# Weight sums in two steps, their loads reordered, and a remainder copy on one engine: a change at the start of a dilated-convolution kernel

## The chip, the cores and the metric

The kernel runs on one core of a Trainium2 chip. The metric is the device time in microseconds (us) of one execution. The engines that compute are TensorE (PE in the profile; PEld is its weight load), VectorE (DVE), ScalarE (ACT) and GpSimd (POOL). SP is the queue from which most DMAs are issued; ACT and POOL issue some as well.

## The reference

A causal convolution with 15 taps at distance 2, from 144 to 288 channels, over two sequences of 16000 steps, then a gate and a projection:

```
xp = pad(x, 28 steps in front)
h  = sum over i of  xp[:, 28 - 2i : 28 - 2i + T, :] @ w[i]      # w: 15 x 144 x 288
z  = tanh(h[..., :144]) * sigmoid(h[..., 144:])
out = z @ w_o                                                   # w_o: 144 x 144
```

All arrays are bf16.

## The kernel before, in words

The channels are split into 128, which fill TensorE's rows, and a remainder of 16. For the 128, the kernel uses a fast-convolution scheme: sums and differences of shifted inputs (tiles S, D, E and their further sums S2, S4, S42, E2, E4 and so on, made by VectorE, L316) are multiplied with sums and differences of weights (tiles G1, Gm, H, HH, GD), so that fewer products are needed. The stationary operand of a matmul is an input tile, the moving operand a weight tile of 288 columns; every product of this kind is recorded at L491. The remainder channels are gathered into a tile R (for taps 0 to 7 and 8 to 14 at once) and multiplied with Wr.

Positions are cut into 11 blocks and 21 units. A unit does four products called S, D, F and G; each has steps VV (with HH), V2 (with H), AV (with GD, for S and D) and A (with the taps themselves and the remainder). ScalarE moves sums between PSUM banks (L677, L683, L695, L761), VectorE combines them into y (L316), ScalarE gates (tanh and sigmoid, L744 and L746), VectorE multiplies (z), a DMA transposes z, and TensorE projects (OP0, OP1; evicted at L882). PSUM is used as four pairs of banks. The first unit's A products of the remainder are separate steps with an r at the end (A11Fr).

The order of every queue is written out by hand in the string ORDER: for PE, ACT, DVE, DMA (which is SP) and POOL, the steps in their order, as unit/name#number, with unit -1 for what is prepared before the first unit. A planner walks these lists and emits the instructions; the costs and due times (want) given to it only settle in which order the queues' instructions are interleaved in the program and which pair of banks each step gets. Instructions that stand in the code outside the planner, such as the clearing of the first xt, xn and Wr tiles on GpSimd (L336, L354, L376, L536), come ahead of all planned steps of their engine.

What matters for the change:

- **Warming.** L525 to L527: NWARM matmuls of 512 columns on zeros (wz), before any data is there.
- **Weight loads.** load_w (L529) loads the 128-channel part of w in four chunks q of four taps (three in the last), on SP, into w_all. Step w is chunk 0, w#1 chunk 1, w#2 chunk 2, w#3 chunk 3; ORDER has them as w, w#2, w#1, w#3, first on SP. After them come the first block's input in two halves (xn, xn#1, L343, transposing DMAs) and its remainder channels in three loads (xt, xt#1, xt#2, L384; the first one is 24 runs of 32 bytes into one partition), with the first xt between the two halves.
- **Weight sums.** For S, psum_sum (L560) adds weights on TensorE: matmuls of the weights with the identity or its negative into PSUM, and a ScalarE copy out (L572). G = w[j] + w[j+8]; H = G[j] - G[j+4]; HH and GD are further differences. Each sum is built directly from w, so HH takes up to eight matmuls for a column block; 59 matmuls in nine groups. For D, F and G the sums are made by VectorE (wsum, L550; instructions at L554).
- **Remainder of the first block.** sums_front (L403): VectorE's st sums (tile T), 16 transposes on TensorE per half block (trR, L420) into a pair of banks, then two copies into R, ScalarE's for one bank and VectorE's for the other (cpR, L427), then two matmuls that zero the banks (zR, L432). This is done twice, for the two units of the block.
- **Wr loads.** 15 loads of 9 KB on POOL (L540), mixed with the loads of w_o (L542, L547, L548) and the clearing of its tile (L544).
- **The end.** The last unit's gates (gate, L730) take smaller pieces: F's four columns at once (th8), then G's first two (th0), then columns 2 and 3 alone (th2, th3), with y made in two instructions for the latter (L788). All pieces under four columns use the start of the same th and sg tile. project_end (L816) transposes z on TensorE (L844), copies it (L855), projects it and evicts it (ose, L852; L830 for columns 4 to 7). store_last (L908) then stores twelve columns, each with a DMA of its own: columns 6 to 11 from POOL, 1 and 3 from ACT, 0, 2, 4 and 5 from SP.

Of the kernel before, what the change touches and what calls it, by code (L numbers as in the profile page):

```python
# [8 lines left out]
BF16 = mybir.dt.bfloat16  # L9
# [17 lines left out]
def t_dve(n, psum=False):  # L27
# [19 lines left out]
   V2bD A00S A01S VVF A00D A01D A10D A11D V2bF V2aF 8/OP0 9/VVG A01F A11F A00F A10F 10/AVS 9/V2bG V2aG 8/OP1 10/VVS 9/A01G A00G 10/AVD V2aS V2bS 9/A10G
   10/VVD 9/A11G 10/A01S V2aD V2bD A00S A10S A11S A11D VVF A10D A01D A00D V2aF V2bF 11/AVD 10/VVG A10F A00F V2aG A11F 9/OP1 10/A01F V2bG 9/OP0 11/VVS
   10/A10G A11G A01G A00G 11/V2aS V2bS AVS VVD A11S A10S V2bD V2aD A00S A01S VVF A10D A11D V2bF V2aF A01D A00D 10/OP0 11/A10F VVG A01F 12/AVS 11/A11F
   A00F V2aG V2bG 10/OP1 12/VVS 11/A00G A01G 12/AVD V2bS V2aS 11/A11G 12/VVD 11/A10G 12/A01S V2bD V2aD A00S A10S A11S A00D VVF A01D A11D A10D V2aF V2bF  # L50
   13/AVD 12/VVG A10F A01F A11F A00F V2bG V2aG 11/OP1 OP0 12/A11G 13/VVS 12/A10G 13/AVS V2bS V2aS 12/A00G 13/VVD 12/A01G 13/A11S V2aD V2bD A10S A00S
   A01S A00D A01D VVF A11D A10D 12/OP0 13/V2bF V2aF VVG 14/AVS 13/A01F V2aG A00F V2bG A10F A11F 12/OP1 13/A00G 14/VVS 13/A01G 14/AVD V2bS V2aS 13/A11G
   14/VVD 13/A10G 14/A01S A00S V2bD V2aD A10S A11S VVF A10D A11D A01D A00D V2bF V2aF 15/AVD 14/VVG A01F V2bG A10F V2aG A11F A00F A10G 13/OP1 OP0
   14/A11G 15/VVS 14/A00G A01G 15/V2bS V2aS AVS VVD A00S A01S V2bD V2aD A11S A10S VVF A10D A11D A00D A01D V2bF V2aF 14/OP0 15/VVG A01F A00F 16/AVS
   15/V2aG A10F V2bG 14/OP1 15/A11F A10G 16/VVS 15/A11G 16/AVD V2bS V2aS 15/A01G A00G 16/VVD A11S A10S V2bD V2aD A01S A00S VVF A10D A11D A01D A00D V2aF
   V2bF 17/AVD 16/VVG A00F V2aG V2bG A01F A11F A10F A00G A01G 15/OP1 OP0 17/VVS 16/A10G A11G 17/V2aS V2bS AVS VVD A11S A10S V2aD V2bD A01S A00S VVF
   A01D A00D A11D A10D V2aF V2bF 16/OP0 17/VVG A00F A01F A10F 18/AVS 17/V2aG V2bG A11F 16/OP1 17/A00G 18/VVS 17/A01G 18/AVD V2bS V2aS 17/A11G A10G
   18/VVD A10S A11S V2aD V2bD A01S VVF A00S A01D A00D A11D A10D V2aF V2bF 19/AVD 18/VVG A01F A00F A11F A10F V2aG V2bG 17/OP1 OP0 18/A00G 19/VVS 18/A01G
   19/AVS V2bS V2aS 18/A11G A10G 19/VVD A10S A11S V2bD V2aD A01S A00S VVF A11D A10D A00D A01D V2aF V2bF 18/OP0 19/VVG A10F A00F A01F 20/AVS 19/V2aG
   V2bG A11F 18/OP1 19/A00G 20/VVS 19/A01G A11G 20/AVD V2aS V2bS 19/A10G 20/VVD A00S V2bD V2aD A01S A11S A10S A01D A00D VVF A11D A10D V2bF V2aF VVG  # L60
   19/OP1 20/A01F A11F A10F V2bG V2aG A00F 19/OP0 20/A00G A01G OP0 OP1 tr#1 A10G A11G OPe#2 tr OPe#1 tr#2 OPe tr#3 tr#4 OPe#4 OPe#3 OPe#5
ACT:
   -1/wsum#7 wsum#13 wsum#5 wsum#11 wsum#17 wsum#9 wsum#3 hc wsum#1 0/cVVF -1/wsum#15 0/cVF cVVG -1/cpR 0/cVG y1F y0F y0G cVVS y1G eAVS cVS -1/cpR#2
   0/ev0S cVVD ev1S eAVD cVD 1/cVVS 0/ev0D 1/cVS 0/ev1D 1/ev0S cVVD eAVD ev1S cVD eAVS cVVF 0/th4 1/ev1D ev0D cVF 0/th0 1/cVVG 0/sg4 sg0 1/cVG 2/eAVS
   cVVS 1/th4 2/cVS 1/sg4 2/eAVD cVVD ev0S ev1S cVD 1/os0 2/cVVF ev1D ev0D cVF cVVG 3/eAVD 1/sg0 2/cVG 1/th0 os1 3/cVVS 2/th4 sg4 3/cVS cVVD eAVS ev1S
   cVD cVVF ev0S ev0D ev1D cVF 2/os0 3/cVVG 2/th0 4/eAVS 3/cVG 2/sg0 3/sg4 4/cVVS 3/th4 2/os1 4/cVS cVVD eAVD ev1S cVD cVVF ev0S ev0D ev1D cVF cVVG
   3/th0 sg0 5/eAVD 4/cVG 3/os1 os0 5/cVVS eAVS cVS 4/sg4 5/cVVD ev1S cVD ev0S cVVF ev0D ev1D cVF 4/os0 th4 th0 5/cVVG 6/eAVS 5/cVG 4/os1 6/cVVS 4/sg0
   5/sg4 6/cVS cVVD eAVD ev1S cVD cVVF ev0S ev1D ev0D cVF 5/th0 6/cVVG 7/eAVD 5/th4 sg0 6/cVG 5/os1 os0 7/cVVS eAVS cVS cVVD 6/sg4 7/cVD ev0S ev1S cVVF
   ev1D ev0D cVF 6/os0 7/cVVG 6/th0 8/eAVS 6/sg0 7/cVG 6/os1 8/cVVS 6/th4 8/eAVD cVS cVVD 7/sg4 8/ev0S cVD cVVF ev1S ev0D ev1D cVF 7/th4 th0 8/cVVG
   7/sg0 9/eAVD 8/cVG 7/os1 os0 8/th4 9/cVVS 8/sg4 9/cVS cVVD eAVS ev1S cVD ev0S cVVF ev0D ev1D cVF 8/sg0 os0 9/cVVG 8/th0 10/eAVS 9/cVG 8/os1 10/cVVS  # L70
# [174 lines left out]
def kernel(  # L245
# [8 lines left out]
    P = 128  # L254
# [148 lines left out]
    def sums_front(want):  # L403
# [7 lines left out]
        for r in range(2):  # L411
# [11 lines left out]
            for h, (eng, c) in enumerate((("ACT", t_act(8 * P)), ("DVE", t_dve(8 * P)))):  # L423
                def cp(h=h, pr=pr, R=R):
                    src = banks[pr.slot][:, h, 0:512].bitcast(BF16)
                    dst = R.tile[:, 2 * h:2 * h + 2].rearrange("p s k n -> p (s k n)")
                    K_(nc.vector.tensor_copy(out=dst, in_=src) if h else nc.scalar.copy(out=dst, in_=src))  # L427
# [569 lines left out]
```

## Time and profile before

| | us |
|---|---|
| Median of 3 runs | 313.51 (313.39 to 313.54) |
| The profiled execution | 313.12 |
| Its span, first to last instruction | 311.3 |
| TensorE busy | 297.5 (96%), 2604 matmuls |
| VectorE busy | 276.5 (89%) |
| ScalarE busy | 269.0 (86%) |
| GpSimd busy | 27.0 (9%) |

Busy time overlaps between engines, and a matmul's end is modelled, so a busy TensorE isn't TensorE at its peak. A timeline row gives the start, the length, the engine, the line, the operation with output and inputs, and in brackets how long the engine was idle before it and who ended that. SPq, ACTq and POOLq rows are issues of DMAs: their length is the time in which the queue was occupied by the issue, not that of the transfer. The stage table gives for each stretch of time the busy time of each engine, the granted clock of TensorE as a share of full speed, and the DMA engines' share.

### The profile page before, as it was taken

Reading aid. Unit: us, or ns where it says so; the run is one execution under the profiler, and the core shown is the slowest. Engines: PE = TensorE matmul, PEld = TensorE weight load, DVE = VectorE, ACT = ScalarE, POOL = GpSimd, SP = SyncE. Lnnn points to the kernel's source line nnn. Section 1 sums busy time; section 2 is a strip of 40 time slices with the busy share of each in tenths; the row PEclk is TensorE's granted clock in tenths of the full one; section 3 lists DMA queues with packets and bytes.
Section 4 is the critical chain, followed back from the end, with each engine's and each line's share of the span. In section 5 each row is a group of like instructions: output and inputs, shape, how many; then the busy total and the mean of one; then the engine's idle time right before and its main releaser. Section 6 shows DMA issues by size and latency. Waiting matters only on the chain.

```text
span 311.3 us, 6703 instructions
## 1 busy us (share of the span) xinstructions
PE 297.5 (96%) x2604; PEld 276.5 (89%) x2604; DVE 276.5 (89%) x393; ACT 269.0 (86%) x449; POOL 27.0 (9%) x63
## 2 busy tenths in 40 slices
PE   8998899999999999999999999999999999999981
PEld 3797789999999999999999999999999999999881
DVE  4878999999999999899999999989996998899861
ACT  1658789998989989999998999989888999989982
POOL 9830500000000000000000000000000000000013
PEclk9999999999999999999999999999999999999997
DMA  7995569597799866986796698455886647254344
GB/s 199 107 127 118 150 67 174 140 115 153 126 162 282 215 159 104 142 199 155 189 210 98 118 181 182 138 127 162 146 187 80 123 141 231 73 128 114 59 170 131
DMA packets 153110, 45.78 MB, mean 147 GB/s; under 512 B 137061, under 2 KB 151701, under 8 KB 153078
## 3 DMA queue, kind: packets, MB, share of 16 engines
q1 hardware_dynamic: 151610, 44.59, 69.6%
q0 software_dynamic: 1216, 0.70, 1.1%
q8 instruction: 20, 0.33, 0.5%
q14 instruction: 12, 0.10, 0.1%
q10 hardware_dynamic: 252, 0.06, 0.1%
HBM read 13.31 MB, written 11.84 MB: 81 GB/s over the span
## 4 chain that ended last, share of the span: by engine, by line
PE 80%; ACT 13%; DVE 3%; issue 3%; DVEq 0%; ACTq 0%
PE acc L491 77%; ACT m L761 4%; ACT acc L683 3%; PE acc L527 2%; ACT acc L677 1%; ACT sg L746 1%; ACT th L744 1%; ACT R L427 1%; DVE D L316 1%; DVE S L316 1%; PE acc L420 1%; DVE y L316 1%; ACT os L882 0%; ACT av L695 0%; ACT osl L852 0%
## 5 line engine op out<-in xcount | busy, mean ns | idle before, releaser
L491 PEld LDWEIGHTS <-E 128*128 128x128 bf16 x882 | 112.2, 145 | 7.9 <-issue 4.0
L491 PE MATMUL acc<-w_all,E 128*128 128x288 bf16 x630 | 101.2, 286 | 1.0 <-ACT acc L683 0.3
L491 PE MATMUL acc<-Wr,R 128*128 128x288 bf16 x336 | 94.9, 286 | 0.0
L316 DVE TENSOR_TENSOR y<-U,acc 128x576 bf16<-128x576 bf16 (+1 forms) x81 | 59.4, 744 | 9.9 <-PE acc L491 6.5
L683 ACT ACTIVATE acc<-acc 128x576 f32<-128x576 f32 x84 | 54.1, 645 | 7.2 <-PE acc L491 4.9
L761 ACT ACTIVATE m<-acc 128x576 bf16<-128x576 f32 x84 | 52.8, 651 | 4.3 <-PE acc L491 2.9
L491 PEld LDWEIGHTS <-S 128*128 128x128 bf16 x378 | 48.2, 137 | 5.2 <-issue 2.4
L491 PEld LDWEIGHTS <-D 128*128 128x128 bf16 x378 | 48.8, 137 | 4.0 <-issue 1.1
L677 ACT ACTIVATE acc<-acc 128x288 f32<-128x288 f32 x84 | 33.7, 401 | 8.0 <-PE acc L491 6.4
L746 ACT ACTIVATE sg<-y 128x576 bf16<-128x576 bf16 (+3 forms) x45 | 38.9, 872 | 0.5 <-DVE y L316 0.4
L744 ACT ACTIVATE th<-y 128x576 bf16<-128x576 bf16 (+3 forms) x45 | 38.9, 871 | 0.2
L882 ACT CAST os<-acc 128x864 bf16<-128x864 f32 x40 | 34.6, 880 | 2.0 <-DVE y L316 0.9
L316 DVE TENSOR_TENSOR m<-m,av 128x1152 bf16<-128x1152 bf16 x42 | 30.5, 753 | 6.5 <-ACT m L761 6.3
L491 PE MATMUL acc<-wo_ab,zT 128*128 128x144 bf16 x480 | 35.2, 226 | 0.1
L491 PEld LDWEIGHTS <-zT 128*128 128x128 bf16 x480 | 32.2, 98 | 1.5 <-issue 0.3
L491 PEld LDWEIGHTS <-R 128*128 128x128 bf16 x336 | 32.8, 98 | 0.2
L491 PE MATMUL acc<-G,S 128*128 128x288 bf16 x147 | 30.3, 286 | 0.4 <-ACT acc L683 0.2
L491 PE MATMUL acc<-Gm,D 128*128 128x288 bf16 x147 | 29.7, 285 | 0.3
L695 ACT ACTIVATE av<-acc 128x576 bf16<-128x576 f32 x42 | 27.2, 648 | 3.0 <-PE acc L491 2.4
L491 PE MATMUL acc<-H,E 128*128 128x288 bf16 x168 | 28.1, 286 | 1.1 <-ACT acc L677 1.1
L316 DVE TENSOR_TENSOR E<-E 128x1792 bf16<-128x1792 bf16 (+1 forms) x22 | 28.1, 1286 | 0.0
L316 DVE TENSOR_TENSOR z<-th,sg 128x576 bf16<-128x576 bf16 (+3 forms) x45 | 25.5, 573 | 2.1 <-ACT sg L746 1.4
(75 smaller groups left out, 330.0 us busy)
## 6 DMA issues: line engine op xcount, KB each, us to landing
R<-q SPq DMA_DIRECT2D x19, 512.0 KB
out_dram<-os SPq DMA_DIRECT2D x8, 864.0 KB
q<-T SPq DMA_DIRECT2D x10, 256.0 KB
out_dram<-os SPq DMA_DIRECT2D x2, 519.8 KB
xt<-in_x_dram SPq DMA_DIRECT2D x6, 156.0 KB
w_all<-in_w_dram SPq DMA_DIRECT2D x3, 288.0 KB
out_dram<-os SPq DMA_DIRECT2D x2, 337.5 KB
zT<-z SPq DMA_TRANSPOSE x20
```

What stands on the lines that cost most here:

```text
L316: return K_(nc.vector.tensor_tensor(out=out_, in0=a, in1=b, op=op))
L420: K_(nc.tensor.transpose(to, ap(st.tile, c, [1, P]), ident[:, 0, :]))
L427: K_(nc.vector.tensor_copy(out=dst, in_=src) if h else nc.scalar.copy(out=dst, in_=src))
L491: K_(nc.tensor.matmul(bank, lhsT=l(), rhs=r, start=start and q == 0, stop=end and q == len(jobs) - 1, skip_group_check=True))
L527: K_(nc.tensor.matmul(banks[i % 4][:, (i // 4) % 2, :], lhsT=wz[:, 0:P], rhs=wz[:], start=True, stop=True))
L677: add("ACT", t_act(D2), lambda: K_(nc.scalar.activation(out=banks[X.slot][:, 1, 0:D2], in_=banks[X.slot][:, 0, 0:D2], func=ACT.Copy, scale ...
L683: s = add("ACT", t_act(2 * D2), lambda: K_(nc.scalar.activation(out=banks[Y.slot][:, :, 0:D2], in_=banks[X.slot][:, :, 0:D2], func=ACT.Cop ...
L695: add("ACT", t_act(2 * D2), lambda: K_(nc.scalar.activation(out=av.tile[:, SPLIT.index(k)], in_=banks[W.slot][:, :, 0:D2], func=ACT.Copy, ...
L744: add("ACT", t_act(n * D, False), lambda: K_(nc.scalar.activation(out=a_, in_=y_[0], func=ACT.Tanh)), r=[*need, y], w=[th], want=t0, name= ...
L746: add("ACT", t_act(n * D, False), lambda: K_(nc.scalar.activation(out=b_, in_=y_[1], func=ACT.Sigmoid)), r=[*need, y], w=[sg], want=t0 + . ...
L761: add("ACT", t_act(2 * D2), lambda pair=pair, i=i, b2=b2: K_(nc.scalar.activation(out=m.tile[:, i, 2 * b2:2 * b2 + 2, :], in_=banks[pair.s ...
L882: K_(nc.scalar.copy(out=dst, in_=banks[pr.slot][:, :, 0:3 * D].rearrange("p h (q d) -> p h q d", d=D)))
```

## The change

- NWARM goes from 15 to 13.
- SP's order starts with the first xt of block 0, then weight chunks 1, 2, 0 and 3; then both halves of xn, one behind the other, then the other xt loads.
- The S sums are built in two steps. G comes first, from w (four groups, 14 matmuls); HH, H and GD are then built from G (five groups, 24 matmuls). Each group of the second step reads what ScalarE copied out in the first.
- VectorE's order at the start: the sums of Gm and H come in another order; ws#6, ws#2, ws#9, ws#7 and ws#10 stand between the first and the second half of E.
- The remainder's copy out of PSUM (cpR) is one VectorE instruction of 2048 elements instead of one of 1024 on each of ScalarE and VectorE.
- On POOL all 15 Wr loads come first, then the clearing and the loads of w_o.
- At the end: columns 2 and 3 of the last G come from one y instruction; gates of under four columns have parts of the th and sg tiles to themselves; column 7 is stored from SP instead of POOL.
- Costs for the planner change, and with them ORDER in all its lists: the middle has the same steps, in places in another order.

```diff
 PE:
-   -1/wsum#10 wsum#6 wsum#12 wsum#4 wsum#16 wsum#8 wsum#2 wsum wsum#14 0/VVF V2bF V2aF VVG -1/trR 0/V2aG V2bG A01F A11F -1/zR 0/A10F A00F A00G A11Fr
+   -1/wsum wsum#4 wsum#2 wsum#6 wsum#8 wsum#10 wsum#12 wsum#14 wsum#16 0/VVF V2bF V2aF VVG -1/trR 0/V2aG V2bG A11F A01F A00F -1/zR 0/A10F A00Fr A11Fr
+   A10Fr A01Fr A10G A01G A11G 1/AVS 0/A11Gr A10Gr A00G VVS A01Gr A00Gr AVS V2aS V2bS -1/trR#1 0/A10S A11S A00S A11Sr A10Sr A01S A00Sr A01Sr -1/zR#1
...
 ACT:
+   -1/wsum#1 wsum#5 wsum#7 wsum#3 hc wsum#11 wsum#9 wsum#13 wsum#15 0/cVVF -1/wsum#17 0/cVF cVVG cVG y0F y1F y1G cVVS y0G eAVS cVS ev1S ev0S cVVD eAVD
...
 DVE:
+   -1/ws ws#5 ws#1 ws#8 E ws#6 ws#2 ws#9 ws#7 ws#10 E#1 E2 ws#3 ws#11 stE stD stS E4 cpR S 1/stE -1/S4 1/stD -1/wr D S2 wr#1 ws#4 1/stS -1/S42 D2 cpR#1
...
 DMA:
-   -1/w w#2 w#1 w#3 xn xt xn#1 xt#1 xt#2 xt#3 xt#4 xt#5 0/xt -1/xn#2 1/T 0/xn 1/q R 2/xt 0/zT 4/xt#4 2/xn 3/T 1/R#1 3/q 1/zT 4/xn 5/T 6/xt#5 xt#2 3/R
+   -1/xt w#2 w#1 w w#3 xn xn#1 xt#1 xt#2 xt#3 xt#5 xt#4 0/xt -1/xn#2 1/T 0/xn 1/q 2/xt 1/R R#1 4/xt#4 0/zT 3/T q 2/xn 4/xt#5 1/zT 3/R#1 4/xt 5/T 6/xt#3
...
-            for h, (eng, c) in enumerate((("ACT", t_act(8 * P)), ("DVE", t_dve(8 * P)))):
...
+            def cp(pr=pr, R=R):
+                src = banks[pr.slot][:, :, 0:512].bitcast(BF16)
+                dst = R.tile[:].rearrange("p (h s) k n -> p h (s k n)", h=2)
+                K_(nc.vector.tensor_copy(out=dst, in_=src))
+
+            add("DVE", 0.07 + 16 * P / 1700, cp, r=[*pr.part], w=[R], pairs=[pr], want=want + 2 + 8 * r, name="cpR")
...
-    NWARM = 15
+    NWARM = 13
...
-    for q in range(4):
+    for q in (0, 2, 1, 3):
         load_w(q)
...
-        psum_sum(HH[:, i], [plus(i, j) + minus(i, j + 4) + minus(i, j + 2) + plus(i, j + 6) for j in range(2)], wall, [gHH[k]], wt)
-        psum_sum(H[:, i, 0:2], [plus(i, j) + minus(i, j + 4) for j in (0, 1)], wall, [gH[k]], wt + .2)
...
+        psum_sum(g[:, 0:2], [plus(i, j) for j in (0, 1)], wa, [gG[k, 0]], wt)
+        psum_sum(g[:, 4:6], [plus(i, j) for j in (4, 5)], wb, [gG[k, 1]], wt + .1)
+        psum_sum(g[:, 2:4], [plus(i, j) for j in (2, 3)], wa, [gG[k, 0]], wt + .2)
+        psum_sum(g[:, 6:7], [plus(i, 6)], wb, [gG[k, 1]], wt + .3)
+        of = lambda j: g[:, j, :] if j < 7 else w_all[:, 7, :]
+        both = [gG[k, 0], gG[k, 1], gw[1]]
+        psum_sum(HH[:, i], [[(0, of(j)), (1, of(j + 4)), (1, of(j + 2)), (0, of(j + 6))] for j in (0, 1)], both, [gHH[k]], wt + .4)
+        psum_sum(H[:, i, 0:2], [[(0, of(j)), (1, of(j + 4))] for j in (0, 1)], both, [gH[k]], wt + .5)
+        psum_sum(H[:, i, 2:4], [[(0, of(j)), (1, of(j + 4))] for j in (2, 3)], both, [gH[k]], wt + .6)
...
+            own = last and n < 4
+            th, sg = (Gen(v[8].gens[0]) if own else v[4 if n == 4 else 8].new(0) for v in (th_b, sg_b))
+            if own:
+                th.tile, sg.tile = (v[8].tiles[0][:, c0:c0 + n, :] for v in (th_b, sg_b))
...
-        store_last(c, os[c // 6], done_[c], len(units) * TU + 4 + q / 4, "POOL" if c > 5 else "ACT" if c in (1, 3) else "DMA")
+        store_last(c, os[c // 6], done_[c], len(units) * TU + 4 + q / 4, "POOL" if c in (6, 8, 9, 10, 11) else "ACT" if c in (1, 3) else "DMA")
```

204 lines of the change are left out of this document (97 added, 107 removed).

## The prediction

> **What bounds the kernel now.** I read the table by stage first, then the timelines of the first 30 us and the last 10, where the diff works.
>
> ```profile
> 26.50:39.75 13.25, 11.04 (x81) 9.40 (x80) 11.89 (x17) 10.59 (x21) 4.73 (x9) 1.00 0.75 151
> ...
> 66.25:278.25 212.00, 211.05 (x1887) 201.77 (x1886) 197.71 (x271) 195.43 (x321) 0.96 (x5) 1.00 0.74 156
> ...
> 303.80:307.20 3.40, 1.17 (x13) 0.62 (x10) 1.05 (x4) 1.60 (x6) 2.43 (x4) 1.00 0.71 224
> 307.20:311.30 4.10, 0.00 (x0) 0.00 (x0) 0.00 (x0) 0.00 (x0) 0.00 (x0) 0.51 0.16 36
> ```
>
> In this table (columns: stretch, length, busy PE, PEld, DVE, ACT, POOL, clock, DMA) TensorE is busy for 211.05 of 212.00 us from 66 to 278 us. There it is full: an edit that gives VectorE or ScalarE time back is worth nothing in that stretch, and a delay at the start is carried to the end unless the loose stages, 13 to 53 us, swallow it (2.2 us idle in 26.5 to 39.75 alone). So the question is when the start hands over to the full stretch. Four timelines of the start, by engine, tell what it waits for (columns: start, length, engine, line, operation, tiles, count, idle before it and who ended it):
>
> ```profile
> 1.19 6.20 PE L527 MATMUL acc<-wz 128*128 128x512 bf16 x15 [1.19 <-DVE wz L521]
> 7.23 7.39 PE L491 MATMUL acc<-w_all,ident 128*128 128x288 bf16 x59
> 14.46 0.41 PE L491 MATMUL acc<-HH,E 128*128 128x288 bf16 x2
> ...
> 17.64 1.14 PE L491 MATMUL acc<-w_all,E 128*128 128x288 bf16 x8
> 19.03 0.41 PE L432 MATMUL acc<-wz 128*128 128x288 bf16 x2 [0.25 <-DVE R L427]
> ```
>
> ```profile
> 0.74 2.11 SPq L531 DMA_DIRECT2D w_all<-in_w_dram  x4
> ...
> 5.65 0.94 SPq L384 DMA_DIRECT2D xt<-in_x_dram  x1
> ```
>
> ```profile
> 1.94 0.61 POOL L376 MEMSET xt<- 128x624 bf16 x1
> ```
>
> ```profile
> 5.87 0.76 DVE L554 TENSOR_TENSOR H<-w_all 128x1152 bf16<-128x1152 bf16 x1 [0.47 <-DMA w_all<-in_w_dram]
> 6.56 0.61 DVE L554 TENSOR_TENSOR Gm<-w_all 128x864 bf16<-128x864 bf16 x1
> 7.20 0.31 DVE L554 TENSOR_TENSOR GD<-Gm 128x288 bf16<-128x288 bf16 x1
> 7.43 0.60 DVE L554 TENSOR_TENSOR H<-w_all 128x864 bf16<-128x864 bf16 x1
> 7.95 0.45 DVE L554 TENSOR_TENSOR HH<-H 128x576 bf16<-128x576 bf16 x1
> 9.33 0.96 DVE L316 TENSOR_TENSOR E<-xn 128x1536 bf16<-128x1536 bf16 x1 [0.93 <-DMA xn<-in_x_dram]
> ...
> 12.29 1.09 DVE L316 TENSOR_TENSOR E<-E 128x1792 bf16<-128x1792 bf16 x1
> ...
> 14.49 0.76 DVE L316 TENSOR_TENSOR T<-xt 128x256 bf16<-128x256 bf16 x3 [0.37 <-issue]
> 15.18 1.48 DVE L316 TENSOR_TENSOR E<-E 128x2560 bf16<-128x2560 bf16 x1
> ```
>
> Now TensorE warms up, sums weights without a gap until 14.46, and the first unit's taps (w_all,E) follow at 17.64, behind the E sums of VectorE, which end at 16.66.
>
> **The loads: a moved step that stalls its queue.** The new order puts the first xt load of block 0 ahead of the weights on SP. It is small (24 runs of 32 bytes), but it writes a tile that GpSimd clears first, and that row ends at 1.94 + 0.61 = 2.55 us. SP issues in order, and now nothing waits there: its weights start at 0.74. After: xt issues at about 2.6, takes the 0.94 of its row, and the weights start at 3.55. That is **+2.8 us** for four weight loads and both halves of xn behind them. For the issue alone there is a second look at that line:
>
> ```profile
> L384 SPq DMA_DIRECT2D xt<-in_x_dram x36: 373/719/3417, 5.6 to 249.4; - x36
> ```
>
> The median is 0.72 and the shortest 0.37, so the shift is 2.3 to 2.9; I take the row of the same load. In return the second xn half has no xt between it and the first, worth at most 0.94 + 0.05 for it alone.
>
> **VectorE.** All starts that waited for a DMA shift: the third weight chunk, by which H began at 5.87, allows sums at 8.7; all four are there by 9.4; the first E half moves from 9.33 to 12.1. Behind it the new order places five sums before the second half. With the spacings of the rows (7.20 to 7.43: 0.23; 7.43 to 7.95: 0.52; HH about 0.37) they are 0.23 + 0.52 + 0.52 + 0.23 + 0.37 = 1.87 us. So E's second half starts at 12.1 + 0.9 + 1.87 = 14.87 and ends, 0.95 later, at 15.8. Before E4 come E2 (1.09), two sums (0.23 + 0.37) and the three st sums (0.69 from 14.49 to 15.18), each overlapping its neighbour a little: E4 starts at 18.0 and ends, 1.48 later, at 19.5.
>
> **Weight sums on TensorE.** The direct sums took 59 matmuls; in two steps they are 14 for G, then 8 + 4 + 4 + 8 = 24, so 38: **21 fewer**, at (14.46 - 7.23)/59 = 0.1225 us each, 2.6 us. Two warming matmuls go as well, but they would end before the weights come. Timeline: eight from 8.7 and six from 9.7, done at 10.4; ScalarE's four copies (some 0.6 each, estimated by size from its row of 1.01 for 1024 elements below; two of them lie beside the matmuls) let the second step start at 11.4; 24 x 0.1225 ends it at 14.4. That is the 14.46 of now. The saved matmuls pay for the late weights and for ScalarE's turn between the steps, nothing more, and the first unit then waits for E until 15.8. The taps start behind E4 at 19.55 against 17.64: **+1.9 us**.
>
> **What the loose stages swallow.** The remainder copies:
>
> ```profile
> 17.24 1.01 ACT L427 COPY R<-acc 128x1024 bf16<-128x1024 bf16 x1
> ```
>
> ```profile
> 18.29 0.69 DVE L427 COPY R<-acc 128x1024 bf16<-128x1024 bf16 x1 [1.63 <-ACT R L427]
> ...
> 23.75 1.35 DVE L316 TENSOR_TENSOR S<-S 128x768 bf16<-128x768 bf16 x2
> ```
>
> ```profile
> 23.68 0.65 PE L491 MATMUL acc<-GD,S 128*128 128x288 bf16 x4
> 24.42 0.69 PE L491 MATMUL acc<-H,S 128*128 128x288 bf16 x4
> ...
> 27.83 0.41 PE L432 MATMUL acc<-wz 128*128 128x288 bf16 x2 [0.77 <-DVE R L427]
> ```
>
> VectorE's half waits for ScalarE's (1.63 idle), since both write R. VectorE alone has no row for 2048 elements: between 0.69 (one half) and 1.4 (two); with 0.6 ns an element and one start, 1.28. The first then ends at 20.8, while TensorE has twelve tap matmuls from 19.55 to 21.0: the wait of 0.25 goes. Between the R copy's end (18.98) and S2's, about 24.4 in the second row, lie 5.4 us of sums; the new order takes a GD sum (0.3) and D4 (1536 elements, as the E half: 0.9) out of them, less overlap 1.0. So S2 comes at 20.7 + 4.4 = 25.1, and TensorE needs it at 25.75; the present gap before 24.42 (0.25, from 23.68 + 4 x 0.1225) goes too. So +1.4. The second copy runs 27.45 to 28.7, and the zeroing matmuls start at 28.75 against 27.83, with twelve tap matmuls ahead of them instead of eight: 0.92 - 0.49 = +0.43. ScalarE has lost two copies of 1.01, but 13 to 40 us is where it had idle time; D4, which the longer copy pushes to 28.7 + 0.9 = 29.6, costs some 0.1 to 0.4, and one ScalarE gate (sg) now stands before two evictions. Followed tile by tile through unit 1 with the same durations, TensorE is 0.3 to 0.6 behind until 48 us, then full. I take **+0.5**, between -0.9 (every wait of 13 to 40 us that is ended by ScalarE or VectorE closes) and +1.9 (nothing is swallowed). Wr's loads first on GpSimd: fifteen of them now come before w_o's instead of among them, so they land earlier, not later, and the last w_o loads stay behind the same later clearing of an xt tile; nothing.
>
> **The middle** is the same work in another order. The table leaves 0.95 us of idle TensorE in 212, the most a better order could win; a worse one can cost more, as a stage like 26 to 40 shows. I take 0, from -0.9 to +0.8.
>
> **The end.**
>
> ```profile
> 304.57 3.56 SPq L914 DMA_DIRECT2D out_dram<-osl  x4
> ```
>
> ```profile
> 303.85 0.69 ACT L830 CAST osl<-acc 128x288 bf16<-128x288 f32 x2
> ...
> 306.18 2.35 ACTq L914 DMA_DIRECT2D out_dram<-osl  x2
> ```
>
> One y instruction for two, gates with tiles of their own, and A11G ahead of the transposes should bring the last ScalarE copies forward, by my following about 1 us, so ScalarE's two stores, last now (306.18 + 2.35 = 308.53), end near 307.4. But SP gets a fifth store. At 3.56/4 = 0.9 each, and with its first one at 304.0, since the copy that it waits for is now the first of the two of L830, which end at 304.54, SP issues until 308.5. The bound moves from ScalarE's queue to SP's: 0, from -0.6 to +0.5.
>
> **Sum.** +0.5 + 0 + 0 on the profiled execution of 313.12 us (span 311.3 and 1.8 around it) gives 313.6. That execution lies 0.39 below the median of 313.51, so on the median **314.0 us**.
>
> [...] TensorE now sits mostly idle from 6.7 to 8.7 and from 10.4 to 11.4. The trace lost its clock (0.51) after 303.80 to 307.20, busy for 1.17 of 3.40; the new stretch of 6.9 to 10.3 holds 14 sums, 1.7 of 3.4, and may or may not. [...] That is the rival Clock.
>
> **Rivals.**
> - Nothing swallowed. The loads' delay goes through whole: 313.51 + 1.9 = 315.4, and more if the middle's order adds to it. For it: SP, VectorE and TensorE all run in order, and my following by hand leaves small waits out. Against: the three gaps named above.
> - Clock (ends slower). If the stretch 6.9 to 10.3 counts as idle, the 24 second-step sums run at 0.24 instead of 0.12 and end at 17.3 instead of 14.4. E4 at 19.5 covers that. If the next window too, with TensorE waiting in it, keeps the clock low until 20.5, the taps lose some 1.3 us: 315.2. It decides from a share between 34% and 50% busy.
> - Hidden (ends faster). ScalarE's 2.0 us of copies and VectorE's wait of 1.63 for the first set the hand-over, not E4; then the delay is swallowed, a wait closes beyond it (-0.5), and the earlier tail counts (-0.3): 312.7. For it: the chain runs through R and S sums from 17 to 28 us. Against: VectorE gets 1.2 us of copies more.
> - It doesn't do what it says: the sums do begin with the weights, but the matmuls saved never reach the path. That is part of my forecast.
>
> **Chances.** A measurement of this kernel tells 0.2%, 0.63 us, from no change. Forecast (313.5 to 314.6) 0.50, Nothing swallowed 0.20, Clock 0.08, Hidden 0.22. Of the forecast 0.34 lies within 0.63 us and 0.16 above; Hidden gives 0.20 faster and 0.02 within. So faster 0.20, same 0.36, slower 0.44. The range reaches to most of Hidden and of the slow rivals: 312.6 to 315.5.
>
> **What would show it.** Right: SP's first weight issue near 3.5 behind xt; E's first half near 12; 38 sums with a gap after the 14th; the first tap near 19.5; the zeroing matmuls with no wait on R; five stores on SP, last at the end. Wrong: weights that start at 0.7 (xt not held by the clearing: about 312); half-clock sums; a middle with under 210 of 212 us busy; ScalarE's stores still last.

## The result, and the profile after

The changed kernel takes **316.45 us** (median of 4 runs, 316.29 to 316.82) against 313.45 (4 runs, 313.37 to 313.54): ratio 1.0093, 95% interval 1.0066 to 1.0119. It is 3.0 us slower, where 0.5 was forecast; the range ended at 315.5. The profiled execution has a span of 314.5 (before 311.3), so 3.2 us have to be found in it.

SP's queue first (start, length of the issue, queue, line, operation, tiles, count):

```profile
2.58 0.93 SPq L384 DMA_DIRECT2D xt<-in_x_dram  x1
3.57 2.11 SPq L531 DMA_DIRECT2D w_all<-in_w_dram  x4
5.72 5.32 SPq L343 DMA_TRANSPOSE xn<-in_x_dram  x2
```

The xt load waits for its tile's clearing, and the weights start at 3.57 for 0.74: 2.83 later. That is the 2.8 of the prediction. GpSimd's clearing ended at 2.55, xt issued at 2.58, and everything behind it on SP stood until then.

TensorE and VectorE in the same stretch:

```profile
1.19 5.47 PE L527 MATMUL acc<-wz 128*128 128x512 bf16 x13 [1.19 <-DVE wz L521]
9.47 3.35 PE L491 MATMUL acc<-w_all,ident 128*128 128x288 bf16 x14 [2.82 <-DMA w_all<-in_w_dram]
...
13.86 0.90 PE L491 MATMUL acc<-G,ident 128*128 128x288 bf16 x6 [0.79 <-ACT G L575]
...
16.55 0.29 PE L491 MATMUL acc<-w_all,ident 128*128 128x288 bf16 x1
17.05 0.47 PE L491 MATMUL acc<-HH,E 128*128 128x288 bf16 x2 [0.22 <-DVE E L316]
...
20.84 1.69 PE L491 MATMUL acc<-w_all,E 128*128 128x288 bf16 x12
22.37 0.41 PE L432 MATMUL acc<-wz 128*128 128x288 bf16 x2
...
30.24 0.41 PE L432 MATMUL acc<-wz 128*128 128x288 bf16 x2
```

```profile
13.32 0.96 DVE L316 TENSOR_TENSOR E<-xn 128x1536 bf16<-128x1536 bf16 x1 [1.35 <-DMA xn<-in_x_dram]
...
19.30 1.48 DVE L316 TENSOR_TENSOR E<-E 128x2560 bf16<-128x2560 bf16 x1
20.70 1.22 DVE L426 COPY R<-acc 128x2048 bf16<-128x2048 bf16 x1
```

The sums begin at 9.47, the first 14 take 3.35 us (0.24 each, at a granted clock of 0.50 from 9.68 to 13.09), the first tap stands at 20.84 for 17.64 (**+3.2**, forecast +1.9), right behind E4, which ends at 19.30 + 1.48 = 20.78. The copy takes 1.22 (forecast 1.28), and the zeroing at 22.37 waits for nothing, as forecast.

Where TensorE gets full, the same place can be found in both kernels: the taps (w_all,E) that follow the pair HH,E between 50 and 60 us. Before, then after:

```profile
53.17 0.41 PE L491 MATMUL acc<-HH,E 128*128 128x288 bf16 x2
53.64 0.65 PE L491 MATMUL acc<-w_all,E 128*128 128x288 bf16 x4
```

```profile
56.02 0.41 PE L491 MATMUL acc<-HH,E 128*128 128x288 bf16 x2
56.49 0.65 PE L491 MATMUL acc<-w_all,E 128*128 128x288 bf16 x4
```

I call this place the mark. It is 2.85 later: from the first tap to it the changed kernel takes 56.49 - 20.84 = 35.65, the old one 53.64 - 17.64 = 36.00. So the stretch is 0.35 shorter, where the forecast had 1.4. The middle is the same (columns as in the first table of the prediction):

```profile
26.50:39.75 13.25, 11.66 (x92) 9.83 (x91) 12.86 (x18) 9.79 (x20) 0.00 (x0) 1.00 0.94 173
...
66.25:278.25 212.00, 211.05 (x1885) 201.44 (x1884) 198.85 (x273) 195.84 (x321) 1.00 (x5) 1.00 0.75 156
```

211.05 busy of 212.00 in both, so the forecast 0 there holds. In the first row VectorE is busy for 12.86 of 13.25, where it had been 11.89. The end, before and after:

```profile
305.29 0.55 PE L491 MATMUL acc<-wo,zt 72*128 72x144 bf16 x6 [0.52 <-DVE zt L855]
...
302.39 3.85 POOL L914 DMA_DIRECT2D out_dram<-osl  x6 [78.93 <-ACT osl L852]
```

```profile
307.65 0.84 PE L491 MATMUL acc<-wo,zt 72*128 72x144 bf16 x8
...
307.33 4.41 SPq L919 DMA_DIRECT2D out_dram<-osl  x5
...
307.89 2.45 POOL L919 DMA_DIRECT2D out_dram<-osl  x4 [0.28 <-ACT osl L857]
309.01 2.30 ACTq L919 DMA_DIRECT2D out_dram<-osl  x2
```

TensorE ends at 308.49 for 305.84, 2.65 later; from there to the end of the span are 6.01 for 5.46 (+0.55). SP's fifth store is the last issue, 311.74, as forecast (whether it sets the end is taken up with the stores below). The sum, first tap, tap to mark, mark to TensorE's end, and the rest: +3.20 - 0.35 - 0.20 + 0.55 = 3.2.

### The profile page after: what moved, and what is told of

The parts are those of the page before. It is cut to its first block, busy times and chain, and to the rows that moved or that the text cites. A ratio compares the mean times of both kernels' runs of the same rounds, so it can differ in the third digit from the quotient of the medians.

```text
span 314.5 us, 6650 instructions
## 1 busy us (share of the span) xinstructions
PE 297.1 (94%) x2581; PEld 274.6 (87%) x2581; DVE 277.2 (88%) x392; ACT 267.2 (85%) x447; POOL 26.3 (8%) x62
## 4 chain that ended last, share of the span: by engine, by line
PE 41%; issue 39%; DVE 7%; ACT 6%; DMA 2%; POOL 2%; SPq 1%; POOLq 0%; ACTq 0%; DVEq 0%
PE acc L491 41%; DMA xn<-in_x_dram 2%; DVE E L316 2%; ACT m L767 2%; ACT acc L686 2%; DVE D L316 1%; POOL out_dram L919 1%; DVE m L316 1%; DVE S L316 1%; ACT acc L680 1%; SPq L531 1%; DVE U L316 0%; DVE y L316 0%; ACT th L750 0%; DVE H L557 0%
## 5 line engine op out<-in xcount | busy, mean ns | idle before, releaser
L316 DVE TENSOR_TENSOR y<-U,acc 128x576 bf16<-128x576 bf16 x80 | 59.1, 751 | 7.7 <-PE acc L491 4.5
```

What stands on the lines that cost most here:

```text
L316: return K_(nc.vector.tensor_tensor(out=out_, in0=a, in1=b, op=op))
```

## The experiments

Theories: **Loads** (the moved xt load makes all late; VectorE's E4 hands it on; the first expectations call it Stall, and Order the rival that the rest of the change loses the time), **Clock** (the starved TensorE gets half clock, 0.50 from 9.68 to 13.09 in after, and its own chain to the first tap gets late), and, on what follows the first tap, **Swallow** against **Carried** (late starts are absorbed by 53 us, or not). "Kept busy" means matmuls on zeros, into PSUM that the next step overwrites, as in a_warm (with nine more ahead of the first unit's VVF; a_xt_back_warm and a_xt_wr_warm keep 13 warming matmuls, since their weights come early):

```diff
-    NWARM = 13
+    NWARM = 24
+    def fill(pr, n):
+        for i in range(n):
+            K_(nc.tensor.matmul(banks[pr.slot][:, 0, :], lhsT=wz[:, 0:P], rhs=wz[:], start=True, stop=True))
...
+            if dst is fill_at[0]:
+                fill(pr, 4)
```

| run | time, us | ratio to before, 95% | sums end | E4 ends | first tap | tap to mark |
|---|---|---|---|---|---|---|
| before | 313.45 | 1 | 14.62 | 16.66 | 17.64 | 36.00 |
| after | 316.45 | 1.0093 (1.0066 to 1.0119) | 16.84 | 20.78 | 20.84 | 35.65 |
| after_again | 316.49 | 1.0115 (1.0096 to 1.0134) | 16.11 | 19.77 | 19.83 | 35.63 |
| b_xt_first | 317.29 | 1.0129 (1.0116 to 1.0142) | 18.64 | 19.88 | 21.65 | 36.00 |
| b_xt_first_warm | 316.41 | 1.0109 (1.0094 to 1.0123) | 17.20 | 19.64 | 20.21 | 36.00 |
| a_xt_back | 314.25 | 1.0027 (1.0011 to 1.0042) | 12.57 | 18.04 | 19.30 | 35.56 |
| a_xt_back_warm | 313.07 | 0.9993 (0.9981 to 1.0005) | 12.50 | 17.90 | 17.96 | 35.65 |
| a_clear_early | 315.37 | 1.0070 (1.0052 to 1.0087) | 13.90 | 19.16 | 20.45 | 35.97 |
| a_warm | 315.79 | 1.0078 (1.0055 to 1.0101) | 15.16 | 20.37 | 20.43 | 35.66 |
| a_wr_mixed | 317.26 | 1.0126 (1.0113 to 1.0139) | 19.10 | 20.16 | 22.11 | 35.56 |
| a_wr_mixed_warm | 315.91 | 1.0087 (1.0062 to 1.0113) | 15.32 | 19.75 | 19.84 | 36.06 |
| a_xt_wr_warm | 313.23 | 1.0006 (0.9987 to 1.0026) | 12.32 | 17.78 | 17.84 | 36.52 |
| b_dve_copy | 312.86 | 0.9974 (0.9955 to 0.9993) | 14.12 | 17.22 | 17.28 | 35.56 |
| a_split_copy | 316.49 | 1.0094 (1.0071 to 1.0118) | 17.76 | 19.84 | 20.77 | 35.78 |
| a_store7 | 317.08 | 1.0116 (1.0089 to 1.0144) | 18.09 | 20.23 | 21.11 | 35.58 |
| c_warm_store7 | 314.19 | 1.0019 (1.0006 to 1.0032) | 12.02 | 17.27 | 17.33 | 35.62 |

The last four columns are from each run's one trace, in us. A time is compared by the ratio, since the kernel before took 312.9 to 313.6 beside the different groups of runs; it needn't equal the quotient of the two medians.

### The moved load

Undone in the changed kernel, done alone in the old one, and with its wait shortened.

```diff
-   -1/xt w#2 w#1 w w#3 xn xn#1 xt#1 ...
+   -1/w#2 w#1 w w#3 xn xt xn#1 xt#1 ...
```

> The changed kernel with one move undone: on SP the first xt load goes back between the two halves of xn; every other queue is as in the changed kernel. Theory Stall (xt waits 1.8 us for the clearing and takes 0.93 us to issue, and the weights wait behind it): weights issue at 0.74 instead of 3.57, the first E half starts near 10.5 instead of 13.32, the first tap near 18 instead of 20.84, and the time falls by 2.3 to 2.8 us, to 313.7 to 314.2. Rival Clock (the half clock from 9.7 to 13.1 is the loss): the late weights are also what idles TensorE, so the time falls, but by under 1 us if the clock still drops. Rival Order (the loss is in the new order of the first units and the fifth store on SP): falls by under 0.5 us, stays above 315.9.

```diff
-   -1/w w#2 w#1 w#3 xn xt xn#1 xt#1 ...
+   -1/xt w w#2 w#1 w#3 xn xn#1 xt#1 ...
```

> The kernel before with one move made: on SP the first xt load stands ahead of the weights, the second xn half directly behind the first; nothing else is changed. Theory Stall: weights issue near 3.57, and with TensorE's 59 direct sums behind them the first unit starts near 7.2 + 2.8 + 7.2 = 17.3 instead of 14.46; most of 2.8 us stays: 315.5 to 316.3. Rival Order: under 0.5 us, 313.4 to 313.9, since the stall alone is swallowed by the loose stages from 13 to 53 us. Rival Clock: TensorE waits with idle from 7.4 to 10, so a half clock can appear here too; it would be seen in the clock column, and would add up to 1.7 us to the stall.

```diff
-    for t_ in xt_b.tiles:
+    for n_, t_ in enumerate(xt_b.tiles):
-        K_(nc.gpsimd.memset(t_[:, (NX - 1) * CR:], 0.0))
+        K_(nc.gpsimd.memset(t_[:, (NX - 1) * CR if n_ else 0:], 0.0))
...
-                z_()
+                if bi:
+                    z_()
```

> The changed kernel with xt still first on SP, but the clearing of its tile moved forward on GpSimd to about 0.74 (end near 1.4 instead of 2.55). A dose test. Theory Stall: xt issues near 1.4 instead of 2.58, all loads 1.15 us earlier, time falls by about 1.0 us, to 315.3 to 315.6; the xt issue itself (0.93) is still paid. Rival Order: no change, 316.2 to 316.7. Rival Clock: TensorE idles 1.15 us less and the half-clock window may go, with it more than 1.15 us.

The load alone costs the old kernel 1.29%, by the medians more than the whole change. Taking it back in the changed kernel brings 0.66%, and clearing the tile earlier, so that xt issues at 1.40 for 2.58, brings 0.23% (its interval overlaps that of after). So Loads has the right cause. But E4 isn't all: in a_clear_early it ended 1.62 earlier than in after (19.16 for 20.78), and the first tap came only 0.39 earlier, for a reason shown below with a_xt_back. And b_xt_first shows a second thing. TensorE, VectorE, and the mark:

```profile
10.02 8.62 PE L491 MATMUL acc<-w_all,ident 128*128 128x288 bf16 x58 [0.21 <-DMA w_all<-in_w_dram]
...
21.65 1.14 PE L491 MATMUL acc<-w_all,E 128*128 128x288 bf16 x8
...
57.65 0.53 PE L491 MATMUL acc<-w_all,E 128*128 128x288 bf16 x3
```

```profile
18.39 1.49 DVE L316 TENSOR_TENSOR E<-E 128x2560 bf16<-128x2560 bf16 x1
```

E4 ends at 19.88, yet the first tap comes at 21.65. What it follows is the end of the sums, 18.64, by 3.01 us: the two VV products and their turn through ScalarE, the V2s and 16 transposes. Before, 14.62 to 17.64 is 3.02 too, with E4 done 0.98 earlier. So the first tap has **two rails**, E4 and TensorE's own chain from the sums, and the old kernel ran on the second. From the tap to the mark it is 36.00, as before: Carried.

In a_xt_back the half clock comes later, while TensorE waits for E: two stretches of 3.41 us, granted 1.00 and 0.50, and the transposes in the second (start and end, length, busy PE, PEld, DVE, ACT, POOL, clock):

```profile
12.44:15.85 3.41, 1.02 (x7) 0.64 (x6) 3.38 (x7) 1.91 (x4) 3.41 (x5) 1.00 1.06 55
15.85:19.26 3.41, 3.41 (x25) 2.68 (x24) 2.76 (x6) 0.94 (x2) 3.41 (x7) 0.50 0.96 79
```

```profile
16.69 1.89 PE L420 MATMUL acc<-ident,T 128*128 128x128 bf16 x16
```

The 16 take 1.89, where after needed 1.07 at full clock, and the tap is 1.26 behind E4: 19.30, where about 18 was expected. In a_clear_early it is the same, 1.89 for the 16 (granted clock 0.87 from 13.25 to 26.50 us) and a tap 1.29 behind E4; there the first twelve taps are slow too (2.01, after 1.69), which is in its 35.97 to the mark.

### GpSimd's loads

Wr's 15 loads among those of w_o, as before:

```diff
-   -1/wrl wrl#1 wrl#2 wrl#3 wrl#4 wrl#5 wrl#6 wrl#7 wrl#8 wrl#9 wrl#10 wrl#11 wrl#12 wrl#13 wrl#14 wz wo72 wol#7 ...
+   -1/wrl wrl#1 wrl#2 wrl#3 wrl#4 wz wol#14 wrl#5 wol#10 wo72 wol#2 wrl#6 wol#13 wrl#7 wrl#8 wol#9 wrl#9 wol#5 ...
```

> The changed kernel with the POOL queue as in the kernel before: five Wr loads, then the clearing of w_o's tile, then Wr and w_o loads mixed; xt still first on SP. The first E half came 4.0 us later than before although the weights issue only 2.83 us later; 1.2 us are open. Theory Wr (11 Wr loads issued from 3.1 to 8.6 share the DMA engines with the weights and xn): the first E half moves from 13.32 to about 12.3, the first tap from 20.84 to near 19.8, the time falls by 0.7 to 1.1 us, to 315.4 to 315.8. Rival (the 1.2 us come from xt, or from both xn halves queued without a gap): no change of E, time 316.2 to 316.7.

E's first half came at 12.37, not 13.32, as expected, and the time still didn't fall, since TensorE was granted 0.60 of its clock from 6.88 to 13.25 us and 0.81 from there to 26.50, and its sums ended at 19.10. That looks like a price of Wr's loads, 0.95, hidden by the clock. But after_again, below, has the same order of loads as after, and E's first half at 12.32 too.

### TensorE kept busy

> The changed kernel, with TensorE kept busy on zeros while it would wait: 24 warming matmuls for 13, four matmuls of 512 columns ahead of the second step of the sums and nine ahead of the first unit's VVF. By Loads, the first tap waits for E4 (20.78 in the changed kernel, first tap 20.84), whose chain hangs on the xn load and not on TensorE: the sums finish by about 15, the first tap stays at 20.7 to 20.9, time 316.2 to 316.6. By Clock, the half clock from 9.7 to 13.1 is on the path: first tap near 19.5, time about 315.2.

> The changed kernel with GpSimd's old order of loads, and with TensorE kept busy on zeros (24 warming matmuls, four ahead of the second step, seven ahead of VVF). Without these it took 317.26, although the first half of E came 0.95 earlier than in the changed kernel, since TensorE's sums ran at half clock until 17. If Wr's loads cost 0.95 at the start and the half clock hid that: E's first half again near 12.4, first tap near 19.9, time 315.3 to 315.6. If GpSimd's order itself costs time later (Wr too late for the remainder's products): 317 again, with TensorE waiting for Wr between 20 and 25.

> The changed kernel with the xt load back between the halves of xn, and TensorE kept busy on zeros (four matmuls ahead of the second step, six ahead of VVF). Without these it took 314.25, with runs from 313.1 to 315.8 and a first tap at 19.30 behind transposes at half clock. By Clock: granted clock 1.00 from 9 to 26 us, first tap near 18.0, time 312.8 to 313.3 and little scatter. If the clock is not what made 314.25: 314 again, scattered as before.

> The changed kernel with both orders of loads as in the kernel before (xt between the halves of xn, GpSimd's list mixed), and TensorE kept busy on zeros (four matmuls ahead of the second step, two ahead of VVF). What is left of the change is the two-step sums, the remainder's copy on VectorE and the end. E's first half should come near 9.4, as before, and the first tap near 17.2 (before: 17.64). If the loads and the clock are the whole loss: 312.3 to 313.2, below the kernel before. If the reordered stages behind them lose as well: 313.8 or more, with TensorE idle for over 4.8 us between 26 and 53.

With the clock at 1.00, the first tap follows E4 by 0.06 to 0.09 us in all four. a_warm, whose tap (20.43) and time lie between its two expectations, gains 0.0015 in the ratio, which the intervals don't separate; a_xt_back_warm gains 0.0034, which they do. With the load back and the clock kept, the changed kernel is level with the old one: the two explain the loss. Level is a balance, though: in the traces a_xt_back_warm still has its first tap 0.32 later and 0.54 more behind TensorE's end, against 0.35 less from tap to mark. a_xt_wr_warm and a_wr_mixed_warm show what Wr first is for, and what else was late. VectorE in each:

```profile
22.86 0.31 DVE L557 TENSOR_TENSOR Wr<-Wr 128x288 bf16<-128x288 bf16 x1 [1.40 <-DMA Wr<-in_w_dram]
```

```profile
22.97 0.43 DVE L316 TENSOR_TENSOR st<-xt 128x512 bf16<-128x512 bf16 x1 [0.95 <-DMA xt<-in_x_dram]
```

With the mixed list and an early start VectorE waits 1.40 for Wr; with the late start the next xt loads, behind the same queue, are late too (0.95). These two are the only runs at full clock in which the tap-to-mark time is above its order's usual. The wait for Wr is one that lateness does fill: a_wr_mixed has the same list, a first tap at 22.11, no wait for Wr and 35.56 to the mark. In time the 1.40 doesn't show (1.0006 against 0.9993 for a_xt_back_warm, intervals overlapping), and a_xt_wr_warm's start was itself later than expected (E's first half at 10.32 for 9.4, the tap at 17.84 for 17.2).

### The copy, and the end

```diff
-            for h, (eng, c) in enumerate((("ACT", t_act(8 * P)), ("DVE", t_dve(8 * P)))):
...
+            def cp(pr=pr, R=R):
+                src = banks[pr.slot][:, :, 0:512].bitcast(BF16)
...
+            add("DVE", 0.07 + 16 * P / 1700, cp, r=[*pr.part], w=[R], pairs=[pr], want=want + 2 + 8 * r, name="cpR")
```

> The kernel before with one edit: the remainder's copy as one VectorE instruction of 2048 elements. VectorE's wait of 1.63 before its half and its half of 0.69 are replaced by about 1.22, so VectorE comes to S about 1.1 earlier (17.8 for 18.90). If VectorE sets the hand-over to the full stretch: 312.4 to 312.7. If Wr's late loads then stop it (wr at 23.53 in the kernel before; Wr not there before about 22.9), or TensorE does: 313.0 to 313.5, with a wait for Wr at the wr sum. The run is also a second look at the old order of loads: E's first half near 9.3 again, if that was no accident.

```diff
-            add("DVE", 0.07 + 16 * P / 1700, cp, r=[*pr.part], w=[R], pairs=[pr], want=want + 2 + 8 * r, name="cpR")
+            first = []
+            for h, (eng, c) in enumerate((("DVE", t_dve(8 * P)), ("ACT", t_act(8 * P)))):
...
+                first = [add(eng, c, cp, r=[pr.part[h]], w=[R], pairs=[pr], want=want + 2 + 8 * r, name="cpR", behind=first)]
```

> The changed kernel with the remainder's copy split again, VectorE's half first and ScalarE's half behind it. VectorE has 0.53 less to do for each unit of the first block. If the late start is carried through because VectorE is full from 13 to 53 us: S starts about 0.5 earlier, and the time falls by 0.5 to 1.0, to 315.4 to 316.0. If VectorE's load there makes no difference, or ScalarE's half and the zeroing behind it come late: 316.3 to 316.8.

The copy alone makes the old kernel faster: 0.9974 (0.9955 to 0.9993). Of the versions run, this is the only one whose interval lies below the old kernel. VectorE and TensorE in it:

```profile
17.14 1.22 DVE L426 COPY R<-acc 128x2048 bf16<-128x2048 bf16 x1
18.28 1.21 DVE L316 TENSOR_TENSOR S<-xn 128x2048 bf16<-128x2048 bf16 x1
```

```profile
17.28 1.21 PE L491 MATMUL acc<-w_all,E 128*128 128x288 bf16 x8
...
26.98 0.40 PE L432 MATMUL acc<-wz 128*128 128x288 bf16 x2 [0.39 <-DVE R L426]
...
52.84 0.65 PE L491 MATMUL acc<-w_all,E 128*128 128x288 bf16 x4
```

VectorE's wait of 1.63 is gone, S starts at 18.28 for 18.90, and tap to mark is 35.56 for 36.00. a_split_copy took 1.06 off VectorE and won nothing, but it settles little: ScalarE's second half ran from 29.36 to 30.37 there, and the second zeroing stood right behind it, at 30.42 for 30.24.

```diff
-        ..., "POOL" if c in (6, 8, 9, 10, 11) else "ACT" if c in (1, 3) else "DMA")
+        ..., "POOL" if c > 5 else "ACT" if c in (1, 3) else "DMA")
```

> The changed kernel with one edit: column 7 is stored from GpSimd again, so SP has four stores at the end and not five. If SP's fifth issue sets the end (SP 311.74, ScalarE's queue 311.31 in the changed kernel), the last issue is ScalarE's and the time falls by 0.3 to 0.5, to about 316.0. If the end hangs on GpSimd's sixth store or on the landing of another: no change or slower, 316.4 to 317.

> The changed kernel with xt between the halves of xn again, with TensorE kept busy on zeros (four matmuls ahead of the second step, six ahead of VVF) and with column 7 stored from GpSimd. Without the last edit it took 313.07 against 313.2 of the kernel before on the same chip. By the sum of the single edits 0.3 to 0.5 less: 312.6 to 312.8 where the kernel before takes 313.2. If the end's stores make no difference: 313.1.

Neither gained the 0.3 to 0.5 that was hoped for. The end of a_store7:

```profile
307.47 4.05 SPq L919 DMA_DIRECT2D out_dram<-osl  x4
...
308.04 3.06 POOL L919 DMA_DIRECT2D out_dram<-osl  x5 [0.28 <-ACT osl L835]
309.16 2.40 ACTq L919 DMA_DIRECT2D out_dram<-osl  x2
```

The last issue on any queue is earlier (311.56 for 311.74), yet from TensorE's end to the span's end are 6.56 for 6.01, and c_warm_store7 against a_xt_back_warm gives 6.61 for 6.00 (ratio 1.0019 for 0.9993, intervals just apart). In this end a sixth store on GpSimd costs more than a fifth on SP. GpSimd's issues fit that: its last one ends at 311.10 here and at 310.34 in after (307.89 + 2.45), and the span ends 4.1 and 4.2 behind it, while it ends 3.6 and 2.8 behind the last issue of the other queues. So in after too the end may hang on GpSimd's last store as much as on SP's; no run took a store away from GpSimd. The old kernel has six there as well, but issues them from 302.39, well ahead of TensorE's end at 305.84.

### The last two

> The kernel before with the first xt load ahead of the weights, and 26 warming matmuls for 15, so that TensorE works nearly until the weights are there. Without the warming it took 317.29, with the sums ending at 18.64 at half clock, E4 at 19.88 and the first tap at 21.65, about 3.0 behind the end of the sums. If the half clock set that tap: sums end near 16.7, the first tap waits for E4 only, near 19.9, 2.3 later than in the kernel before, and the time is 315.5 to 315.9. If the loads alone make the 3.9: first tap 21.6 again, time 317.3.

> The changed kernel once more, for the spread of its start. By two rails (E4 behind the xn load, and TensorE's own chain of about 3.0 from the end of the sums, lengthened by the half clock), the first tap lies between 20.5 and 21.2 whichever comes last, and the time is 316 to 317. If the late xn of the first look (13.32 for E's first half) is a property of the kernel, it comes at 13.2 to 13.4 again; if it is scatter, between 12.3 and 13.0.

With 26 warming matmuls for 15, b_xt_first_warm ran its sums at full clock (granted 1.00 from 6.88 to 26.50 us; b_xt_first had 0.73 from 6.88 to 13.25), but they still end at 17.20, not at the expected 16.7, since the last chunk of w came at 9.93. So the first tap, 1.44 earlier, is again 3.01 behind the sums and not behind E4; tap to mark again 36.00. The gain in time is 0.0020 of the ratio, less than the tap's, and the intervals overlap a little (in the traces 0.50 of the 1.44 is lost again between the mark and TensorE's end, 252.70 for 252.20): that the half clock set b_xt_first's tap is shown by the trace, its price in time only roughly. after_again has E's first half at 12.32, in the range named for scatter, and the tap at 19.83, earlier than the expected 20.5 to 21.2, in its profiled execution, which took 315.23; its five times go from there to 317.41. So the late xn of after's trace was scatter.

## Why the prediction was wrong, step by step

Of the 2.7 us that the profiled execution takes more than forecast (3.2 for 0.5), the first tap has 1.3, the swallowing 1.05, the end 0.35.

- **Stalled queue, +2.8 on SP: right** (2.83). The loads behind it were forecast from it rightly as well: E's first half at 12.1, measured 12.3 to 13.3 in the traces with this start.
- **"The taps start behind E4 at 19.55", +1.9: too small; measured +2.2 (after_again) to +3.5 (a_store7).** The best case was taken for the likely one. The working read the old tap of 17.64 as "behind the E sums of VectorE, which end at 16.66"; the 0.98 between was TensorE's own 3.02 from the end of the sums. So the rival Clock was mis-sized where it said "E4 at 19.5 covers that": sums that end at 17.3 put the tap at 17.3 + 3.0 = 20.3. This is what a_split_copy (17.76, then 20.77) and a_store7 (18.09, then 21.11) show; in after it was E4 behind a late xn, 20.78. It was said that the rival "decides from a share between 34% and 50% busy"; the window ahead of the sums was busy for 0.60 of 3.42 in after (last section). The 34% is the 1.17 of 3.40 ahead of the one change of the clock in the old trace, the 50% an estimate for 14 sums. How long a half clock lasts ("until 20.5") was an estimate too, since the old trace ends in its half clock; it lasted 3.41 in after and 6.83 in a_store7.
- **"What the loose stages swallow": 0.35 for 1.4, and even the 0.35 isn't lateness swallowed.** The gaps named did close: from the first tap to the second zeroing (30.24, before 27.83) lateness went from 3.20 to 2.41 with four more matmuls (0.49) done, so 1.28 were gone, against 1.47 forecast. But between there and the mark 0.93 came back, which the working ("Followed tile by tile through unit 1 ... 0.3 to 0.6 behind until 48 us") had at about nothing. It came back at once: from the second zeroing to the second pair HH,D behind it the changed kernel takes 7.52 (37.76 - 30.24) for 43 matmuls, the old one 6.96 (34.79 - 27.83) for 47. TensorE's waits behind the second zeroing, the two longest of after, what ScalarE waited for ahead of the first of them, then that pair HH,D and the longest wait of before:

```profile
37.76 0.41 PE L491 MATMUL acc<-HH,D 128*128 128x288 bf16 x2 [0.43 <-ACT m L767]
...
40.35 0.41 PE L491 MATMUL acc<-Gm,D 128*128 128x288 bf16 x2 [0.68 <-ACT acc L686]
```

```profile
37.05 0.65 ACT L767 ACTIVATE m<-acc 128x576 bf16<-128x576 f32 x1 [1.04 <-PE acc L491]
```

```profile
34.79 0.41 PE L491 MATMUL acc<-HH,D 128*128 128x288 bf16 x2
...
36.84 0.41 PE L491 MATMUL acc<-HH,E 128*128 128x288 bf16 x2 [0.45 <-ACT m L761]
```

  The two of after are ended by ScalarE, which itself waited for TensorE until 37.05 and then had no idle time up to 40.30: a loop that starts late as a whole. An idle gap like that holds nothing that lateness could use. In the old order, taps at 17.64, 20.21 and 21.65 gave 36.00 to the mark each time. What is shorter in the new order is shorter whatever the lateness: in the eight traces that have its copy, taps at full clock and no wait for a load behind them, with first taps from 17.33 (c_warm_store7) to 22.11 (a_wr_mixed), it is 35.56 to 35.66 to the mark, and each time 9.3 to 9.4 of it up to the second zeroing and 7.52 from there to HH,D. So the 1.28 and the 0.93 both belong to the order of the steps, and the late start went through whole. b_dve_copy gets 35.56 from the copy alone. Which of the moved steps gives the 0.93 back is open. It isn't the copy by itself: from the second zeroing to HH,D b_dve_copy takes 7.01, and a_split_copy 7.60. (In the working of S2, "TensorE needs it at 25.75" is 25.8 by its own terms, which changes nothing.)
- **The copy, 1.28: 1.22, right.** A row for 2048 elements, which the working missed, was there, though of another operation: S<-xn at 18.90 in the old trace, 1.22 too.
- **Weight sums: right in count and in the gap, without use.** 38 matmuls with ScalarE's turn of 0.79 between; but E, not the sums, set the first unit where the clock was full.
- **Wr first: "nothing": right here**, with a wait of 1.40 at stake where the start isn't late (a_xt_wr_warm).
- **The middle, 0: right. The end, 0: measured +0.35** (-0.20 from the mark to TensorE's end, +0.55 behind it), inside its bounds. The -0.20 is of the new order: 251.9 to 252.1 from mark to TensorE's end in all its traces, 252.2 to 252.7 in the old order. The fifth store is the last issue, as named, but "the bound moves from ScalarE's queue to SP's" isn't shown, as GpSimd's last store fits the end as well; a sixth on GpSimd would have been worse.
- **Rivals.** "Nothing swallowed" (315.4) was held at 0.20 and "Clock" at 0.08, as alternatives. Both came, in part, and they add: a first tap later than 19.55 (by the half clock in a_store7, 0.50 from 10.49 to 17.32, and in a_split_copy, 0.74 from 6.88 to 13.25 and 0.87 from there to 26.50; by a late xn in after) and no swallowing. The range had no case for the two together.

## What to carry to other kernels

Before a delay is called swallowed, follow each wait in the loose stage to an anchor: here the wait for Wr's loads, which stayed where they were, took lateness up, and the waits between TensorE and ScalarE, which all started late, took up none. A step may have a second rail one engine away; measure the distance from both (here E4 + 0.06 and the sums' end + 3.01), since the edit that delayed one here starved the other. And when a bundle loses, try its parts in the old kernel: here one line of load order cost 1.3%, and another edit of the same change was a gain of 0.26%.

## What the runs showed of the hardware

Near the start, TensorE's clock was granted at 0.50 for 3.41 us in after (9.68 to 13.09) and for 6.83 in a_store7 (10.49 to 17.32), with the same order of loads and sums. After and a_store7, with a stretch of the same length on either side:

```profile
6.26:9.68 3.42, 0.60 (x4) 0.28 (x3) 0.15 (x1) 0.00 (x0) 2.77 (x6) 1.00 1.23 260
9.68:13.09 3.41, 3.39 (x15) 1.92 (x14) 2.26 (x4) 1.50 (x3) 2.49 (x5) 0.50 1.06 216
13.09:16.50 3.41, 2.64 (x22) 2.12 (x22) 3.18 (x7) 2.15 (x6) 3.41 (x6) 1.00 1.14 69
```

```profile
7.08:10.49 3.41, 1.04 (x9) 0.84 (x9) 0.95 (x2) 0.36 (x1) 2.42 (x6) 1.00 1.16 252
10.49:13.91 3.42, 2.63 (x12) 1.46 (x11) 2.59 (x6) 2.10 (x5) 3.08 (x5) 0.50 1.10 179
13.91:17.32 3.41, 3.41 (x16) 2.08 (x15) 3.38 (x7) 1.46 (x3) 3.41 (x7) 0.50 1.12 72
17.32:20.73 3.41, 2.86 (x31) 2.57 (x30) 2.91 (x7) 2.79 (x6) 3.41 (x7) 1.00 0.85 73
```

The stretch with 0.60 us of matmuls in after and the one with 1.04 (30%) in a_store7 are followed by half clock, as are 1.02 of 3.41 in a_xt_back and 1.17 of 3.40 at the end of before. After's half-clock stretch was busy for 3.39, and behind it the clock is full again; a_store7's first was busy for 2.63 and is followed by a second, busy for 3.41 and followed by full clock. The 2.63 is 3.42 less the gap of 0.79 for ScalarE's turn between the two steps of the sums, from 12.23 to 13.02 there; in after the gap goes from 13.07 to 13.86, and the clock rises at 13.09. That this gap cost a_store7 its second stretch is my estimate from these rows; no run moved the gap alone. What was measured: the same start has its sums end at 16.11 (after_again, granted 0.73 from 6.88 to 13.25 and 1.00 from there to 26.50), 16.84 (after) or 18.09 (a_store7).
